# A new order of all engines, mask copies moved, fillers of 256 columns, the last product in two halves

## The chip, the cores and the metric

The kernel runs on one core of one Trainium2 chip. The metric is device time in microseconds (us), the median of the runs shown. Before the change it is 151.94 us, the median of three runs (150.77 to 152.38).

The engines have short names here: PE is TensorE (matrix products, with weight loads on their own row as PEld), DVE is VectorE, ACT is ScalarE, POOL is GpSimd, SP is SyncE. SP only issues transfers (DMAs) in this kernel. [...]

## The reference

Two stages follow each other. The first is linear attention with decay, for 4 batches, 8 heads, 768 positions and head dimension 64. In float32:

```python
for b in range(nb):                                   # blocks of 64 positions
    intra = einsum('bhic,bhjc->bhij', qb, kb) * Dmask  # Dmask[i, j] = lam ** (i - j), 0 above
    intra = einsum('bhij,bhjd->bhid', intra, vb)
    inter = einsum('bhid,bhde->bhie', qb * lam_pow, kv_state)
    out[:, :, sl] = intra + inter
    kv_state = lam_block * kv_state + einsum('bhsd,bhse->bhde', kb * rev_pow, vb)
```

The second is a gated feed-forward layer over the 512 features of each position:

```python
h = maximum(x @ w_in, 0)              # w_in is 512 x 1024
u, v = h[..., :512], h[..., 512:]
v_n = (v - mean(v)) / sqrt(var(v) + 1e-06)
v_s = einsum('ts,bsd->btd', w_spatial, v_n) + b_spatial[None, :, None]   # 768 x 768
out = (u * v_s) @ w_out               # w_out is 512 x 512
```

## The kernel before

**Tiling.** The 768 positions of a batch are three blocks of 256; with four batches there are twelve blocks, numbered 0 to 11. A block has all eight heads. Within a block, c is one of two chunks of 128 positions. The decay is split into factors of q and of v: `lq`, `lqn` and `lv` are tables of powers of lam, made at the start on ACT (LX, LT) from logarithms, so that the mask is only zeros and ones (`m01`).

**Steps.** A step is a short function; the string `ORDER` at the top lists all of them by token. A token has a name, its arguments, and a last letter for the engine: T for TensorE, D for DVE, A for ACT, P for POOL, S for SP. The steps for block n are:

- LK, LQ, LV load k, q and v of the block (512 KB each) through SP's queue. Each has three buffers, so load n goes to buffer n modulo 3 and waits until that buffer's earlier contents have been read.
- KC, QC cast k and q to bfloat16; VD multiplies v by its decay, one half of the heads in VD.n.0 and the other in VD.n.1.
- TK, TQ transpose k and q on TensorE by way of an identity matrix (line 328, eight products of 128 columns); EK, EQ take the results out of PSUM. For blocks 8 to 11, DK and DQ do this by transposing transfers, and QM stands for QC.
- SC makes scores (line 369, sixteen 64x64 products of 128 columns), MK masks them into `a_sb` (line 373, DVE).
- KV adds a chunk to the running state (line 385, sixteen products of 64 columns; it needs both halves of VD), SS copies the state out.
- AV makes the attention output of a chunk (lines 406 and 415); EX copies it out as `xT`. SY is a copy of two elements that keeps two engines apart.
- PV and PU multiply by the v half and the u half of w_in (line 444, four products of 512 columns; line 490, eight of 256); EV and EU are the relu. BN, RA, RD, VN normalise.
- WT transposes w_spatial once (line 502), EW copies it out. It needs all of w_spatial.
- PW multiplies by w_spatial for a batch (line 511, six products of 384 columns); GB adds the bias (line 516); GM multiplies by u (line 522) into `gT`.
- PO multiplies by w_out (line 528, four products of 512 columns), EO copies to one of four `o_sb` slots, ST stores. For the last tile of the last batch the copy and the store are in halves (EH, SH; line 541).
- WU are fillers: products of a constant tile whose result is never read (line 212). WU.24 is 24 of them. They stand on TensorE where it would wait.

**Weights.** w_in, w_spatial and w_out are loaded by POOL's queue (WI.0 the v half and WI.1 the u half of w_in, WS.0 and WS.1 of w_spatial, WO), with a cast to bfloat16 on the way. Ahead of each stands a gate GT.x.n: POOL copies one element out of buffer n modulo 3 of k, q or v (x = 0, 1, 2), and so can't go on until that buffer is loaded:

```python
def after(e, x, n):
    nc.gpsimd.tensor_copy(out=seen, in_=(k_in, q_in, v_in)[x][n % NIN][0:1, H - 1, 0, 0:1])
```

**Order.** There is no loop: the kernel walks through `ORDER` and calls each step. Waits between engines are put in by the framework from what each step reads and writes. The order was written by a planner, with fillers where it left TensorE idle. So the order of the tokens is both each engine's queue and the order in which reads and writes of one buffer are tied to each other.

Of the kernel before, what the change touches and what calls it, by code (L numbers as in the profile page):

```python
# [16 lines left out]
LK.0.2.S lam.A pos.P LQ.0.2.S LV.0.2.S LK.1.2.S msk.P WU.-8.T LB.5.T LN.5.A LL.D idn.P LQ.1.2.S LX.A LT.0.A  # L17
KC.0.2.P LV.1.2.S WU.24.T TK.0.4.T QC.0.2.D EK.0.4.A WU.10.T TQ.0.5.T LQ.2.2.S LT.1.A EQ.0.5.D GT.2.0.P WI.0.P
mkc.D WU.12.T SC.0.1.2.T LK.2.2.S SC.0.0.0.T VD.0.0.P MK.0.1.2.D KC.1.2.A VD.0.1.P MK.0.0.0.D LV.2.2.S WU.21.T
TK.1.2.T QC.1.2.D EK.1.2.D WU.11.T TQ.1.6.T AV.0.0.3.T LK.3.2.S EQ.1.6.D WU.4.T KV.0.0.T SS.0.0.A WU.2.T  # L20
SC.1.0.0.T VD.1.1.P SC.1.1.5.T LT.2.A AV.0.1.3.T MK.1.0.0.D KV.0.1.T GT.1.0.P WI.1.P MK.1.1.5.D VD.1.0.P
SS.0.1.A EX.0.1.4.A EX.0.0.3.D LQ.3.2.S WU.23.T AV.1.0.0.T KV.1.0.T PV.0.1.5.T QC.2.2.A SS.1.0.D LQ.4.2.S
WU.3.T TQ.2.4.T EV.0.1.5.A AV.1.1.0.T EQ.2.4.D GT.0.2.P WS.0.P KC.2.2.A PV.0.0.3.T EX.1.0.0.D GT.2.1.P WS.1.P
EX.1.1.1.A TK.2.2.T BN.0.1.D EV.0.0.3.A PV.1.1.6.T EK.2.2.D KV.1.1.T BN.0.0.D EV.1.1.6.A SC.2.1.0.T SC.2.0.4.T
PV.1.0.3.T LK.4.2.S MK.2.1.0.D RA.0.A VD.2.1.P MK.2.0.4.D WU.9.T PU.0.0.6.T SS.1.1.A VD.2.0.P EV.1.0.3.A
PU.0.1.0.T BN.1.0.D AV.2.0.1.T EU.0.1.0.A RD.0.D BN.1.1.D WU.4.T KV.2.0.T PU.1.0.3.T SS.2.0.A BS.S VN.0.0.A
AV.2.1.1.T KC.3.2.P PU.1.1.4.T EX.2.0.1.D EX.2.1.2.A EU.1.0.3.A EU.0.0.6.D PV.2.1.0.T RA.1.A EU.1.1.4.A
RD.1.0.D TK.3.3.T VN.0.1.D EV.2.1.0.A VN.1.0.D PV.2.0.1.T VN.1.1.D EK.3.3.A BN.2.1.D PU.2.0.4.T LV.3.2.S
EV.2.0.1.A BN.2.0.D EU.2.0.4.A QC.3.2.P WT.4.3.T WT.0.0.T LK.5.2.S EW.4.3.A WT.2.2.T EW.0.0.D WT.5.4.T
EW.2.2.A WT.3.6.T QC.4.2.P EW.5.4.D WT.1.5.T TQ.3.1.T RA.2.A EW.3.6.A LQ.6.2.S RD.2.0.D PU.2.1.3.T EQ.3.1.D  # L30
EW.1.5.A TQ.4.6.T VN.2.0.D EU.2.1.3.A VN.2.1.D SC.3.1.4.T LQ.5.2.S EQ.4.6.D KC.4.2.A SC.3.0.0.T PW.0.1.1.2.T
MK.3.0.0.D PW.0.0.0.3.T LV.4.2.S GB.0.1.1.2.D MK.3.1.4.D TK.4.0.T GM.0.1.1.P PW.0.1.0.6.T VD.3.1.P
GB.0.0.0.3.D LK.6.2.S PW.0.0.1.2.T GB.0.1.0.6.D GM.0.0.0.P EK.4.0.D PW.0.3.1.6.T VD.3.0.P PW.0.2.0.4.T
GB.0.3.1.6.D GM.0.1.0.P LV.6.2.S GB.0.0.1.2.D KV.3.0.T GB.0.2.0.4.D LV.5.2.S AV.3.0.0.T GM.0.0.1.P SC.4.1.2.T
SS.3.0.A SC.4.0.5.T SY.3.0.D AV.3.1.0.T MK.4.0.5.D QC.5.2.P KV.3.1.T PW.0.3.0.4.T EX.3.1.1.A LQ.7.2.S
EX.3.0.0.A MK.4.1.2.D KC.5.2.A TQ.5.6.T VD.4.0.P PU.3.0.5.T EQ.5.6.D LK.7.2.S TK.5.2.T VD.4.1.P SS.3.1.D
EU.3.0.5.A PU.3.1.6.T GB.0.3.0.4.D EK.5.2.A QC.6.2.P KV.4.0.T EU.3.1.6.D AV.4.0.0.T LV.7.2.S SS.4.0.A
SC.5.1.2.T GT.1.1.P WO.P SC.5.0.4.T SY.4.0.A KV.4.1.T AV.4.1.0.T MK.5.0.4.D PV.3.1.6.T KC.6.2.P EX.4.1.1.A
LK.8.2.S EX.4.0.0.A MK.5.1.2.D PW.0.2.1.1.T EV.3.1.6.A VD.5.1.P TK.6.4.T LQ.8.2.S TQ.6.5.T GM.0.3.0.P EK.6.4.D
PV.4.1.6.T EQ.6.5.D QC.7.2.A VD.5.0.P PU.4.1.0.T BN.3.1.D EV.4.1.6.A VD.6.1.P PU.4.0.2.T GB.0.2.1.1.D SS.4.1.A  # L40
EU.4.1.0.A BN.4.1.D VD.6.0.P PV.3.0.6.T EU.4.0.2.A LQ.9.2.S KV.5.0.T GM.0.2.0.P EV.3.0.6.D AV.5.0.0.T SS.5.0.A
SC.6.1.2.T SC.6.0.4.T SY.5.0.D KC.7.2.D KV.6.0.T AV.5.1.0.T PV.4.0.6.T MK.6.0.4.D EX.5.0.0.A EX.5.1.1.A
TK.7.0.T MK.6.1.2.D EV.4.0.6.A PO.0.1.1.T VD.7.1.P EK.7.0.A BN.3.0.D PV.5.1.4.T GM.0.3.1.P EO.0.1.1.A BN.4.0.D
PV.5.0.5.T RA.3.A ST.0.1.S EV.5.1.4.A VD.7.0.P LV.8.2.S RD.3.0.D PU.5.1.6.T EV.5.0.5.A GM.0.2.1.P TQ.7.3.T
BN.5.0.D EU.5.1.6.A PO.0.0.5.T QM.8.1.P SS.6.0.A BN.5.1.D PO.0.2.4.T EO.0.0.5.A EQ.7.3.D RA.5.A AV.6.0.0.T
ST.0.0.S VN.3.0.D EO.0.2.4.A KV.6.1.T LK.10.2.S SC.7.0.5.T SY.6.0.D RD.5.0.D SC.7.1.2.T SS.6.1.A KC.8.2.P
LK.9.2.S AV.6.1.0.T MK.7.0.5.D RA.4.A KV.7.0.T PO.0.5.4.T LV.9.2.S EX.6.0.0.A EX.6.1.1.A QM.8.0.P MK.7.1.2.D
PU.5.0.0.T SS.7.0.A VD.8.1.P RD.4.D KV.7.1.T EU.5.0.0.A AV.7.0.1.T PO.0.3.5.T VD.8.0.P VN.5.1.D VN.4.1.A
PV.6.0.0.T SY.7.1.A LV.11.2.S VN.4.0.D VN.5.0.D PV.6.1.6.T LQ.10.2.S EV.6.0.0.A SS.7.1.D VN.3.1.D EO.0.3.5.A
AV.7.1.1.T KV.8.0.T ST.0.3.S PW.1.0.1.5.T EX.7.1.2.A DQ.8.S EV.6.1.6.A EX.7.0.1.A PW.1.1.1.0.T VD.9.1.P  # L50
BN.6.1.D EO.0.5.4.A DK.8.S PV.7.1.6.T VD.9.0.P GB.1.1.1.0.D BN.6.0.D PU.6.1.2.T QM.9.0.P GB.1.0.1.5.D RA.6.A
PU.7.1.4.T EV.7.1.6.A QM.9.1.P KC.9.2.A BN.7.1.D PU.7.0.1.T SS.8.0.A GM.1.1.1.D PV.7.0.6.T DK.9.S EU.7.1.4.D
PW.1.3.1.3.T RD.6.D EV.7.0.6.A ST.0.2.S EU.6.1.2.A DQ.9.S QM.10.0.P BN.7.0.D PO.0.4.4.T EU.7.0.1.A
GB.1.3.1.3.D VN.6.1.A PW.1.0.0.6.T GM.1.0.1.P ST.0.5.S EO.0.4.4.D RA.7.A PU.6.0.5.T GB.1.0.0.6.D RD.7.D
SC.8.0.3.T LV.10.2.S GM.1.0.0.P EU.6.0.5.A KV.9.0.T SC.8.1.0.T MK.8.0.3.D LQ.11.2.S PW.1.2.1.6.T SS.9.0.A
QM.10.1.P MK.8.1.0.D PW.1.1.0.2.T GM.1.3.1.P PW.1.2.0.4.T GB.1.2.1.6.D GB.1.1.0.2.D AV.8.0.0.T GM.1.1.0.P
GB.1.2.0.4.D SC.9.1.2.T KV.9.1.T SY.8.0.D SC.9.0.5.T MK.9.1.2.D AV.8.1.0.T GM.1.2.1.P PW.1.3.0.4.T EX.8.0.0.A
DQ.10.S GM.1.2.0.P EX.8.1.1.D VN.7.0.A PO.1.3.0.T GB.1.3.0.4.D VN.7.1.A LK.11.2.S PV.8.1.1.T GM.1.3.0.P
VN.6.0.A PV.8.0.4.T EO.1.3.0.A VD.10.1.P EV.8.1.1.A ST.1.3.S PO.1.0.2.T QM.11.1.P EV.8.0.4.A BN.8.1.D
PO.1.1.1.T EO.1.0.2.A VD.10.0.P BN.8.0.D PO.1.5.0.T MK.9.0.5.D QM.11.0.P RA.8.A EO.1.1.1.A PU.8.0.3.T  # L60
KC.10.2.A ST.1.1.S RD.8.D ST.1.0.S PU.8.1.4.T VN.8.0.D ST.0.4.S VN.8.1.A DK.10.S PO.1.4.6.T EU.8.1.4.A
PW.2.0.1.1.T EU.8.0.3.A SS.9.1.A EO.1.5.0.A PW.2.1.1.3.T GB.2.0.1.1.D ST.1.5.S GM.2.0.1.P PW.2.0.0.2.T
GB.2.1.1.3.D KC.11.2.D GM.2.1.1.P PO.1.2.5.T GB.2.0.0.2.D DK.11.S PW.2.2.1.4.T EO.1.2.5.A GM.2.0.0.P
EO.1.4.6.A AV.9.0.0.T KV.10.0.T ST.1.4.S SC.10.1.2.T SY.9.0.D GB.2.2.1.4.D SC.10.0.5.T SS.10.0.A AV.9.1.0.T
# [12 lines left out]
GB.3.2.0.3.D ST.2.5.S ST.2.4.S GM.3.2.0.D PW.3.3.1.4.T GB.3.2.1.2.D PO.3.1.6.T GM.3.2.1.D GB.3.3.1.4.D
PO.3.0.3.T EO.3.1.6.A GM.3.3.1.P PO.3.2.1.T ST.3.1.S EO.3.0.3.A PO.3.5.2.T ST.3.0.S EO.3.2.1.A PO.3.3.5.T
ST.3.2.S EO.3.5.2.A PO.3.4.6.T EO.3.3.5.A ST.3.5.S ST.3.3.S EH.3.4.6.0.A EH.3.4.6.1.D SH.3.4.0.A SH.3.4.1.S
"""  # L80


@with_exitstack
def kernel(
    ctx: ExitStack,
    tc: tile.TileContext,
    q: bass.AP,
    k: bass.AP,
# [9 lines left out]
    P = 128  # L98
# [147 lines left out]
    def c_mask2(e):  # L246
        for c in range(2):
            rows = slice(c * Q64, (c + 1) * Q64)
            nc.vector.tensor_copy(out=m01[rows], in_=mfull[rows, :, :, rows])  # L249
# [335 lines left out]
```

## Time and profile before

| What | Before |
|---|---|
| median of three runs | 151.94 us (150.77 to 152.38) |
| the profiled execution, its own time | 153.37 us |
| its span, first to last instruction | 151.6 us |
| busy TensorE, DVE, ACT, POOL | 139.0, 101.3, 86.0, 79.6 us |
| DMA moved, mean rate over the span | 30.74 MB, 203 GB/s |
| TensorE instructions: products, weight loads | 2157, 2157 |
| of these products, fillers | 131 |
| first WT product starts | 38.08 us |
| last PO group starts | 142.63 us |

Lines of the timeline give the start in us from the beginning of the span, the time to the end of the group in us, the engine, the line of the kernel, the operation, what it writes and reads, the tile sizes and types, and how many instructions were merged. In brackets stand the idle time of the engine ahead of the group and what ended it. `ps` is PSUM, used in eight banks; the last argument of most TensorE tokens is the bank.

### The profile page before, as it was taken

What the parts mean: (1) busy time and instruction counts of PE and PEld (TensorE: products, weight loads), DVE (VectorE), ACT (ScalarE), POOL (GpSimd) and SP (SyncE); (2) the same over time, 40 slices, a digit from 0 to 9 for tenths busy, and PEclk for the clock granted to TensorE, in tenths of its full rate; (3) what the DMA queues carried; (4) which work ended last, traced back from release to release, by engine and by line L of the source; (5) the groups of instructions that cost most, each with busy time, mean ns of one, the idle gap of its engine ahead of it and who ended that gap; (6) DMA issues with size and microseconds to landing.
All of it is one profiled execution on the core that took longest, in us unless ns stands there. A gap on an engine that the chain in (4) does not pass through costs nothing.

```text
span 151.6 us, 5030 instructions
## 1 busy us (share of the span) xinstructions
PE 139.0 (92%) x2157; PEld 94.3 (62%) x2157; DVE 101.3 (67%) x189; ACT 86.0 (57%) x160; POOL 79.6 (52%) x90
## 2 busy tenths in 40 slices
PE   7795787999999995999999999899999999999990
PEld 6794675676975773776655756646576757555540
DVE  2159575958797964887893899946569828725601
ACT  6780356759940664658858562298353739760261
POOL 7464634505029959949370967695478050019310
PEclk9999999999999999999999999999999999999999
DMA  3999999999999799983799999587757000006355
GB/s 95 299 290 254 282 254 279 218 227 311 299 289 251 207 292 263 273 221 91 207 280 270 238 263 244 158 158 268 198 147 134 6 4 2 0 36 241 143 208 208
DMA packets 52041, 30.74 MB, mean 203 GB/s; under 512 B 9522, under 2 KB 48946, under 8 KB 52018
## 3 DMA queue, kind: packets, MB, share of 16 engines
q1 hardware_dynamic: 49488, 27.53, 68.8%
q0 software_dynamic: 2384, 2.75, 10.5%
q8 instruction: 17, 0.28, 0.8%
q10 hardware_dynamic: 146, 0.13, 0.3%
q14 instruction: 6, 0.05, 0.1%
HBM read 24.77 MB, written 6.29 MB: 205 GB/s over the span
## 4 chain that ended last, share of the span: by engine, by line
PE 74%; DVE 13%; DMA 3%; issue 3%; ACT 2%; POOL 2%; DVEq 0%; ACTq 0%
PE ps L511 16%; PE ps L528 13%; PE ps L444 13%; PE ps L490 12%; PE ps L328 5%; DVE a_sb L373 3%; PE ps L415 3%; DMA k_in<-in_k_dram 3%; PE ps L369 3%; PE ps L385 3%; PE ps L212 3%; DVE vsb L516 2%; PE ps L406 2%; PE ps L502 1%; DVE m L249 1%
## 5 line engine op out<-in xcount | busy, mean ns | idle before, releaser
L522 POOL TENSOR_TENSOR gT<-vsb,uT 128x384 bf16<-128x384 f32 x28 | 30.5, 1110 | 32.9 <-DVE vsb L516 20.1
L511 PE MATMUL ps<-wt_sb,vn 128*128 128x384 bf16 x192 | 33.9, 327 | 0.0
L314 POOL TENSOR_TENSOR vd<-v_in,lv 128x512 bf16<-128x512 f32 x24 | 24.8, 1046 | 12.3 <-PE ps L511 5.0
L373 DVE TENSOR_TENSOR a_sb<-ps,m 128x1024 bf16<-128x1024 f32 x24 | 28.5, 1216 | 2.7 <-PE ps L369 2.5
L511 PEld LDWEIGHTS <-vn 128*128 128x128 bf16 x192 | 18.2, 98 | 12.9
L444 PE MATMUL ps<-win_sb,xT 128*128 128x512 bf16 x96 | 24.1, 380 | 2.1 <-DVE a_sb L373 2.1
L516 DVE TENSOR_TENSOR vsb<-ps,bsp 128x384 f32<-128x384 f32 x32 | 17.3, 549 | 10.5 <-PE ps L511 7.2
L490 PE MATMUL ps<-xT,win_sb 128*128 128x256 bf16 x192 | 23.8, 273 | 0.0
L528 PE MATMUL ps<-wout_sb,gT 128*128 128x512 bf16 x96 | 22.9, 380 | 0.0
L459 DVE BATCH_NORM_STATS2 st<-vh 128x6 f32<-128x512 bf16 x24 | 16.4, 684 | 9.3 <-ACT vh L449 9.1
L490 PEld LDWEIGHTS <-win_sb 128*128 128x128 bf16 x192 | 18.4, 98 | 4.3
L449 ACT ACTIVATE vh<-ps 128x512 bf16<-128x512 f32 x23 | 13.7, 596 | 12.0 <-PE ps L444 11.8
L174 ACT ACTIVATE o_sb<-ps 128x512 f32<-128x512 f32 (+1 forms) x23 | 13.2, 587 | 12.5 <-PE ps L528 11.9
L174 ACT ACTIVATE xT<-ps 128x512 bf16<-128x512 f32 x18 | 10.2, 596 | 11.0 <-PE ps L415 11.0
L444 PEld LDWEIGHTS <-xT 128*128 128x128 bf16 x96 | 8.8, 98 | 10.5 <-issue 2.3
L528 PEld LDWEIGHTS <-gT 128*128 128x128 bf16 x96 | 9.0, 98 | 9.5
L449 ACT ACTIVATE uT<-ps 128x512 bf16<-128x512 f32 x21 | 12.2, 596 | 4.7 <-PE ps L490 4.6
L174 ACT ACTIVATE s_sb<-ps 128x256 bf16<-128x256 f32 x16 | 6.1, 381 | 14.3 <-PE ps L385 14.2
L212 PE MATMUL ps<-warm 128*128 128x128 bf16 x131 | 12.0, 255 | 2.1 <-DVE warm L210 1.1
L212 PEld LDWEIGHTS <-warm 128*128 128x128 bf16 x131 | 10.3, 117 | 2.9 <-DVE warm L210 1.1
L415 PE MATMUL ps<-a_sb,vd 64*64 64x128 bf16 x384 | 10.5, 218 | 1.0 <-issue 1.0
L369 PE MATMUL ps<-qT,kT 64*64 64x128 bf16 x384 | 8.8, 218 | 0.4 <-DVE vsb L516 0.4
(71 smaller groups left out, 172.8 us busy)
## 6 DMA issues: line engine op xcount, KB each, us to landing
k_in<-in_k_dram SPq DMA_DIRECT2D x12, 512.0 KB, 7.2
q_in<-in_q_dram SPq DMA_DIRECT2D x12, 512.0 KB, 8.1
v_in<-in_v_dram SPq DMA_DIRECT2D x12, 512.0 KB, 6.7
out_dram<-o_sb SPq DMA_DIRECT2D x23, 256.0 KB, 2.3
wsp_raw<-in_moe_w_spatial_dram POOLq DMA_DIRECT2D x2, 576.0 KB, 11.2
win_sb<-in_moe_w_in_dram POOLq DMA_DIRECT2D x2, 512.0 KB, 9.6
wout_sb<-in_moe_w_out_dram POOLq DMA_DIRECT2D x1, 512.0 KB, 7.8
bsp<-in_moe_b_spatial_dram SPq DMA_DIRECT2D x1, 384.0 KB, 8.2
```

Of the source, the lines that this page charges most:

```text
L174: nc.scalar.activation(out=o, in_=i, func=AF.Copy)
L212: nc.tensor.matmul(out=bank(SB)[:, 4 * D:4 * D + P], lhsT=warm, rhs=warm, start=(n < 0 and x == 0), stop=True, skip_group_check=True)
L314: vec(e).tensor_tensor(out=vd[n % NCA].rearrange("p (o i w) m d -> p o i (w m) d", o=2, i=2)[o], in0=v_in[n % NIN].rearrange("p (o i w) m ...
L373: nc.vector.tensor_tensor(out=a_sb[n % NA][:, i].rearrange("p o w j x -> p (o w) (j x)"), in0=bank(b, 2).rearrange("p o (w y) -> p (o w) y ...
L444: nc.tensor.matmul(out=bank(b), lhsT=x[:, c, g], rhs=win_sb[:, g, DH:DFF], start=(g == 0), stop=(g == NCH - 1))
L449: nc.scalar.activation(out=o, in_=i, func=AF.Relu)
L459: nc.vector.bn_stats(out=st6[p2][:, t], in_=vh[p2][:, t])
L490: nc.tensor.matmul(out=pu[:, f2].rearrange("p (c x) -> p c x", c=2), lhsT=win_sb[:, g, f * P:(f + 1) * P], rhs=x[:, :, g, :], start=(g == ...
L511: nc.tensor.matmul(out=bank(b)[:, 0:HW], lhsT=vn[bb % 2][:, s, f * P:(f + 1) * P], rhs=wt_sb[:, s, i * HW:(i + 1) * HW], start=(s == 0), s ...
L516: nc.vector.tensor_tensor(out=vsb[(bb * 4 + f) % NVS][:, i * HW:(i + 1) * HW], in0=bank(b)[:, 0:HW], in1=bsp[:, i * HW:(i + 1) * HW], op=A ...
L522: vec(e).tensor_tensor(out=gT[bb % 2][:, f, cols].rearrange("p (a y m) -> p a y m", m=2, y=Q64), in0=vsb[(bb * 4 + f) % NVS][:, cols].rear ...
L528: nc.tensor.matmul(out=bank(b), lhsT=gT[bb % 2][:, f, t * P:(t + 1) * P], rhs=wout_sb[:, f, :], start=(f == 0), stop=(f == NCH - 1))
```

## The change

All of `ORDER` is replaced by another order of the same computation; the sets of products on TensorE ahead of the first WT are the same. The head of it, old and new:

```diff
-LK.0.2.S lam.A pos.P LQ.0.2.S LV.0.2.S LK.1.2.S msk.P WU.-8.T LB.5.T LN.5.A LL.D idn.P LQ.1.2.S LX.A LT.0.A
-KC.0.2.P LV.1.2.S WU.24.T TK.0.4.T QC.0.2.D EK.0.4.A WU.10.T TQ.0.5.T LQ.2.2.S LT.1.A EQ.0.5.D GT.2.0.P WI.0.P
-mkc.D WU.12.T SC.0.1.2.T LK.2.2.S SC.0.0.0.T VD.0.0.P MK.0.1.2.D KC.1.2.A VD.0.1.P MK.0.0.0.D LV.2.2.S WU.21.T
-TK.1.2.T QC.1.2.D EK.1.2.D WU.11.T TQ.1.6.T AV.0.0.3.T LK.3.2.S EQ.1.6.D WU.4.T KV.0.0.T SS.0.0.A WU.2.T
-SC.1.0.0.T VD.1.1.P SC.1.1.5.T LT.2.A AV.0.1.3.T MK.1.0.0.D KV.0.1.T GT.1.0.P WI.1.P MK.1.1.5.D VD.1.0.P
-SS.0.1.A EX.0.1.4.A EX.0.0.3.D LQ.3.2.S WU.23.T AV.1.0.0.T KV.1.0.T PV.0.1.5.T QC.2.2.A SS.1.0.D LQ.4.2.S
-WU.3.T TQ.2.4.T EV.0.1.5.A AV.1.1.0.T EQ.2.4.D GT.0.2.P WS.0.P KC.2.2.A PV.0.0.3.T EX.1.0.0.D GT.2.1.P WS.1.P
...
+LK.0.2.S lam.A pos.P LQ.0.2.S LK.1.2.S LQ.1.2.S WU.-8.T LB.4.T LN.4.A LL.D LX.A LV.0.2.S LT.0.A KC.0.2.P
+LV.1.2.S idn.P LT.1.A WU.25.T TK.0.5.T QC.0.2.P msk.P LK.2.2.S EK.0.5.A WU.4.T TQ.0.4.T EQ.0.4.D GT.1.0.P
+WI.0.P mkc.A KC.1.2.D LQ.2.2.S WU.6.T SC.0.0.1.T SC.0.1.5.T TK.1.3.T MK.0.0.1.D QC.1.2.P EK.1.3.A LV.2.2.S
+WU.5.T TQ.1.0.T LT.2.A VD.0.0.D VD.0.1.P EQ.1.0.D LK.3.2.S MK.0.1.5.D WU.9.T SC.1.0.0.T KV.0.0.T VD.1.0.P
+SS.0.0.A MK.1.0.0.D WU.3.T SC.1.1.5.T AV.0.0.3.T GT.0.0.P WI.1.P KV.0.1.T SS.0.1.A SY.0.3.D MK.1.1.5.D
+VD.1.1.P WU.3.T AV.0.1.3.T KV.1.0.T EX.0.0.3.A AV.1.0.1.T LQ.3.2.S SS.1.0.A SY.1.1.D EX.0.1.4.A WU.2.T
+KV.1.1.T AV.1.1.1.T KC.2.2.P EX.1.1.2.A WU.2.T PV.0.1.3.T LQ.4.2.S EX.1.0.1.A GT.0.2.P WS.0.P TK.2.0.T
+EV.0.1.3.A QC.2.2.D PV.0.0.5.T GT.2.1.P WS.1.P EK.2.0.A BN.0.1.D TQ.2.1.T PV.1.1.6.T EV.0.0.5.D EQ.2.1.D
...
```

The crowded part on TensorE around the fourth and fifth block, and the end, in the new order:

```diff
...
+PU.3.0.0.T GB.0.3.0.4.D VD.4.1.P EQ.5.2.D TK.5.5.T EU.3.0.0.A PU.3.1.6.T GM.0.2.0.P LQ.7.2.S EK.5.5.A KV.4.0.T
+GT.0.1.P WO.P AV.4.0.0.T EU.3.1.6.A SS.4.0.D SC.5.0.4.T SY.4.0.A QC.6.2.P LV.7.2.S SC.5.1.2.T KV.4.1.T
+MK.5.0.4.D AV.4.1.0.T PV.3.1.6.T EX.4.0.0.A LK.8.2.S MK.5.1.2.D EX.4.1.1.A PV.3.0.4.T EV.3.1.6.A VD.5.1.P
...
+ST.3.0.S EO.3.2.6.A PO.3.3.4.T ST.3.2.S EO.3.5.5.A PH.3.4.0.0.T PH.3.4.1.1.T EO.3.3.4.A ST.3.5.S ST.3.3.S
+EH.3.4.0.0.A EH.3.4.1.1.D SH.3.4.0.A SH.3.4.1.S
```

In numbers of steps: fillers go from 131 in twelve groups to 71 in eleven. EK moves from four on DVE and four on ACT to eight on ACT; EX on DVE goes from six to two; KC on ACT from six to three; GM on DVE from four to seven (POOL 28 to 25); VD on DVE from none to two. The weights' gates change from GT.2.0, GT.1.0, GT.0.2, GT.2.1, GT.1.1 to GT.1.0, GT.0.0, GT.0.2, GT.2.1, GT.0.1, for WI.0, WI.1, WS.0, WS.1 and WO.

The functions that change:

```diff
-    warm = sb([P, P], BF16, "warm")
+    warm = sb([P, T2], BF16, "warm")
...
-            nc.tensor.matmul(out=bank(SB)[:, 4 * D:4 * D + P], lhsT=warm, rhs=warm, start=(n < 0 and x == 0), stop=True,
+            nc.tensor.matmul(out=bank(SB)[:, 4 * D:8 * D], lhsT=warm[:, 0:P], rhs=warm, start=(n < 0 and x == 0), stop=True,
                              skip_group_check=True)
...
     def c_mask(e):
+        nc.gpsimd.memset(eps_t, 1e-6)
         nc.gpsimd.memset(mfull, 1.0)
...
             rows = slice(c * Q64, (c + 1) * Q64)
-            nc.vector.tensor_copy(out=m01[rows], in_=mfull[rows, :, :, rows])
-        nc.vector.memset(eps_t, 1e-6)
+            copy(e, m01[rows], mfull[rows, :, :, rows])
...
+    def p_h(e, bb, t, b, x):
+        half = slice(x * (DM // 2), (x + 1) * (DM // 2))
+        for f in range(NCH):
+            nc.tensor.matmul(out=bank(b)[:, half], lhsT=gT[bb % 2][:, f, t * P:(t + 1) * P],
+                             rhs=wout_sb[:, f, half], start=(f == 0), stop=(f == NCH - 1))
+
```

The mask copies (mkc) are now on ACT, behind the copy of the first kT. The last tile's product is made by PH in two halves, in banks 0 and 1, and EH copies each half from its own bank.

## The prediction

> **What bounds the kernel now.** I read the page's shares of the engines first, then stretches of the span, then TensorE in order of time, then GpSimd. Page, parts 1 to 3:
>
> ```profile
> PE 139.0 (92%) x2157; PEld 94.3 (62%) x2157; DVE 101.3 (67%) x189; ACT 86.0 (57%) x160; POOL 79.6 (52%) x90
> ...
> DMA  3999999999999799983799999587757000006355
> ...
> q8 instruction: 17, 0.28, 0.8%
> ```
>
> TensorE (PE) is busy 92% of the span; the DMA engines are at nine tenths from the second to the thirteenth slice (to 49 us). The stretches before and after the transposes of w_spatial (steps WT) are the natural cut: both orders put the same products of TensorE ahead of WT.
>
> ```profile
> 0.00:38.08 38.08, 31.75 (x565) 25.36 (x565) 23.58 (x43) 23.43 (x42) 18.29 (x30) 1.00 1.08 251
> 38.08:151.60 113.52, 107.22 (x1593) 68.95 (x1592) 77.72 (x147) 62.58 (x118) 61.30 (x60) 1.00 0.71 187
> ```
>
> (Columns: length; busy us and count of PE, weight loads, DVE, ACT, POOL; clock; DMA share; GB/s.) After WT, TensorE is nearly dense. The head is loose: seven transposing steps at 0.45 us, six SC and five KV at 0.24, six AV at 0.46, six PV and five PU at 0.87, durations from the chain's rows, make 18 us of 38. TensorE in order of time:
>
> ```profile
> 10.75 1.35 PE L212 MATMUL ps<-warm 128*128 128x128 bf16 x21
> ...
> 19.82 1.44 PE L212 MATMUL ps<-warm 128*128 128x128 bf16 x23 [0.48 <-ACT s_sb L174]
> ...
> 21.55 0.41 PE L385 MATMUL ps<-vd,kc 64*64 64x64 bf16 x16
> ...
> 24.81 0.41 PE L415 MATMUL ps<-a_sb,vd 64*64 64x128 bf16 x13 [0.97 <-issue]
> ...
> 58.60 1.04 PE L444 MATMUL ps<-win_sb,xT 128*128 128x512 bf16 x4 [2.12 <-DVE a_sb L373]
> ...
> 96.23 0.42 PE L369 MATMUL ps<-qT,kT 64*64 64x128 bf16 x16 [0.40 <-DVE vsb L516]
> ```
>
> The reader sees three late stops. The first two are of one kind, although the second is put down to DVE. Counting TensorE's instructions in order of start, 707 precede the first stop and 1987 the second[...]. The packet records of queue q8 show 16,384-byte fetches at 22.38 (0.97 us long) and 55.98 (1.19 us); each stop ends 1.45 us after its fetch. These are waits for **instruction fetch**, 3.09 us together. 21.55 is the second block's first KV product, the milestone used below. GpSimd:
>
> ```profile
> 15.11 0.64 POOL L253 COPY seen<-q_in 1x1 f32<-1x1 f32 x1
> 15.70 0.80 POOL L257 DMA_DIRECT2D win_sb<-in_moe_w_in_dram  x1
> 16.51 1.06 POOL L314 TENSOR_TENSOR vd<-v_in,lv 128x512 bf16<-128x512 f32 x1
> 21.17 0.17 POOL L253 COPY seen<-k_in 1x1 f32<-1x1 f32 x1 [3.60 <-DMA k_in<-in_k_dram]
> ...
> 56.74 0.18 POOL L253 COPY seen<-q_in 1x1 f32<-1x1 f32 x1 [1.82 <-DMA q_in<-in_q_dram]
> ```
>
> A gate (GT, line 253) is a copy of one element on GpSimd that holds a weight load back. The last line is the gate GT.1.1 of buffer q_in_1. Loads 1, 4 and 7 use that buffer; load 7 stands ahead of the gate in the order, and the trace's landing of load 7 is at 56.69. So **a gate waits for the last load of its buffer that stands ahead of it**, not for the load whose number it bears.
>
> [...] fillers stand 107 ns apart up to about 10.6 us, 4.4 us after dense work began at 6.2, and 63 ns in the row at 19.82. [...] loads land 1.8 us apart, but 5.19 us apart (14.05, 19.24) where w_in's first half flows.
>
> **The change part by part.**
>
> *Fillers.* 131 of 128 columns become 71 of 256. At 63 ns before and an estimated 109 ns (256/128 of 54 ns, the gap less a few ns) that is 8.2 against 7.7 us, and 120 instructions fewer. They fill waits, so their price on the path is nothing while data is what the head waits for; uncovered, it is 0.5 us less.
>
> *Mask copies to ScalarE, eps memset to GpSimd.* Two copies took 2.12 us on DVE ("DVE m L249", mean 1052 ns), ahead of the first masked scores (12.14). On ACT the nearest row is 0.38 us (s_sb, 128x256); bounds 0.38 to 1.05 each. With k0 ready on GpSimd at 6.15, both lq tables on ACT ahead of kT (4 x 0.42 us each, to about 8.8), kT at 9.8 and the mask at 10.6, the first MK starts at 10.65: 1.5 us earlier.
>
> *Loads.* k1, q1 go ahead of v0, which lands fifth (12.29, not 8.67). Then VD.0 ends about 13.4, KV.0.0 about 14.0, AV.0.1 about 16.9: a lead over before of some 2 to 3 us.
>
> *The gates.* Now the step that decides. The second half of w_in (WI.1) sat behind GT.1.0 (q0, long landed). It is put behind GT.0.0, buffer k_in_0, and LK.3 (load k3, same buffer) stands ahead of it. By the rule above it waits for **k3**, the tenth load. Without WI.1 between them: 14.05 (sixth) + 4 x 1.8 + 3.39 us for w_in's first half = 24.6. Behind the gate on GpSimd stand WI.1's issue and VD.1.1, half of the second block's scaled v, which KV.1.0 needs[...]. 24.65 + 0.18 (gate) + 0.87 (issue, L257 mean 865 ns) + 1.05 (L314) = 26.75 for KV.1.0, against 21.55: 5.2 us later, after 9.8 us of idle TensorE. KC.2 and both w_spatial issues follow on the same queue.
>
> From KV.1.0 to WT the new order has: 3 KV 0.72, 4 AV 1.84, 6 PV 5.22, 3 transposing steps 1.35, 2 SC 0.48, 5 PU 4.37, 8 fillers 0.88 = 14.9 us (durations from the chain's rows; a PV of four 0.87, a PU of eight 0.87, eight transposes 0.45). The cold array adds: the 64-wide steps first, some 1.8 us, hardly slow (32 scores took 0.57 us cold at 10.18); then 2.6 us at half rate lose 1.3, say 1.4. Bounds 0 to 2.2. WT at 26.75 + 14.9 + 1.4 = **43.0**, not 38.08. The data allow it: WI.1 issued at 24.8 lands 9.2 to 10.0 us later as both halves did before (34 to 34.9; first PU about 35.3), and the w_spatial halves, 7.9 us of flow behind it, about 41.6 to 42.4.
>
> *After WT.* Products are the same; 113.5 us less what goes. The fetch stop at 58.6: the crowded run KV.4 to AV.4.1 is still there[...] I take a stop of 0.3, bounds 0 to 2. So -2.12 + 0.3. The stop of 0.40 goes (SC.9 uses other banks): -0.40. Unsized new waits of an order untried: +0.7, bounds 0 to 2.
>
> *Engine swaps and store order.* By counts times means ACT gains about 3 us, DVE loses as much; at 57% and 67% neither becomes the bound, TensorE's products cover them. In SP's queue DK, DQ and the stores change places by one or two entries; stores are waited for by four o_sb slots alone, 0.4 us in all before. Cost nothing; if the cover is gone, each late read of a bank costs its 0.6 us.
>
> *Last product in halves (PH).* Eight matmuls of 256, about 0.44 us a half, for four of 512, 0.87: equal on TensorE. ACT and DVE now read different banks. Before, DVE's half (148.47) waited for ACT's (148.06); at 97.5 the two write one xT tile from different banks at once, so the bank was the reason: -0.45, bounds 0 and -0.6.
>
> Sum against the profiled span: 43.0 + 113.5 - 2.12 + 0.3 - 0.40 + 0.7 - 0.45 = 154.5, or +2.9 on 151.6. That execution took 153.37, 1.77 around its span and 1.43 over the median of 151.94. Added to the median: **154.8 us**, own range 153 to 156.5.
>
> **Rivals.** (A) *The gate is no wait* (faster): GT.0.0 finds k0 landed. Then WI.1 and w_spatial are issued as early as before, land about 35.2, WT comes at 35.5 instead of 43.0: 154.8 - 7.5 = 147.3. For it: too few fillers (2 and 2) stand round KV.1.0 for a 10 us hole. Against: the row at 56.74. It decides if GT.0.0 ends under 20 us. (B) *Fetch stops move instead of going, and the cold lasts*: +2 [...] +0.8 cold: 157. [...] (C) *The head loses less and the rest gains more*: WT at 41.6, when the last w_spatial lands, no new waits: 154.8 - 1.4 - 0.7 - 0.3 = 152.4, about no change.
>
> **Chances.** Main 0.65, A 0.11, B 0.13, C 0.11. A measurement here tells about 1% from nothing, 1.5 us. Slower by over that (from 153.5): main but for its lower edge, and B, 0.75; within: C and that edge, 0.13; faster: A and a little, 0.12. The range leaves out A and B's far end: 150.8 to 157.8.
>
> **What would show it.** In the changed profile: the copy at line 253 waiting for k_in until 24 to 25; PE idle about 9 us before a KV product near 26.8; PV rows with doubled spacing after it; WT near 43; no stop of 2 us in the middle; the two last o_sb copies side by side. Wrong if the gate ends early, or if the stretch after WT is longer than 113.

## The result and the profile after

The changed kernel takes **158.81 us** (median of four runs, 157.76 to 159.15) against 152.04 us (four runs, 150.77 to 152.38) for the kernel before: a ratio of **1.045 [1.037, 1.053]**. It is slower, as forecast, but 4.0 us above the forecast of 154.8 and 1.0 us above the end of its range (157.8). The profiled execution took 158.55 us, its span 156.8. (Ratios here leave disturbed executions out, so they need not be the quotient of the medians beside them.)

The page of the changed kernel, parts 1 to 3 (engines; clock granted to TensorE in 40 slices; DMA in the same slices; the queue of instruction fetches):

```profile
PE 138.6 (88%) x2088; PEld 92.9 (59%) x2101; DVE 99.5 (63%) x191; ACT 88.1 (56%) x166; POOL 77.4 (49%) x88
...
PEclk9999975599999999999999999999999999999999
DMA  4999999999987359999399999972949200035155
...
q8 instruction: 16, 0.26, 0.7%
```

TensorE is busy as long as before in a span 5.2 us longer. Its clock row, all nines before, now has three low slices (7, 5 and 5 tenths), from 19.6 to 31.4 us. The two stretches, cut at the first WT product (columns as in the prediction):

```profile
0.00:44.67 44.67, 32.16 (x503) 23.52 (x505) 20.16 (x39) 24.27 (x46) 20.00 (x33) 0.89 1.06 247
44.67:156.80 112.13, 106.41 (x1587) 69.40 (x1596) 79.39 (x153) 63.81 (x121) 57.41 (x55) 1.00 0.70 176
```

So the head costs 6.59 us more (44.67 for 38.08), and everything after it 1.39 less (112.13 for 113.52). The loss is all ahead of WT. TensorE in order of time:

```profile
18.36 0.29 PE L386 MATMUL ps<-vd,kc 64*64 64x64 bf16 x8
27.70 0.32 PE L386 MATMUL ps<-vd,kc 64*64 64x64 bf16 x5 [9.05 <-POOL vd L315]
...
36.66 1.91 PE L491 MATMUL ps<-xT,win_sb 128*128 128x256 bf16 x16
...
44.67 2.20 PE L503 MATMUL ps<-ident,wsp_raw 128*64 128x128 bf16 x72
...
71.30 0.25 PE L386 MATMUL ps<-vd,kc 64*64 64x64 bf16 x5 [0.66 <-POOL vd L315]
...
81.48 1.47 PE L529 MATMUL ps<-wout_sb,gT 128*128 128x512 bf16 x6 [0.36 <-issue]
```

Half of KV.1.0's sixteen products run at 18.36. The other half needs VD.1.1 and starts at 27.70, after 9.05 us of idle TensorE. The stops of 2.12 and 0.40 us of the kernel before are gone; 0.66 and 0.36 have come. GpSimd shows what VD.1.1 stood behind:

```profile
14.03 1.04 POOL L315 TENSOR_TENSOR vd<-v_in,lv 128x512 bf16<-128x512 f32 x1 [0.66 <-DMA v_in<-in_v_dram]
25.30 0.18 POOL L254 COPY seen<-k_in 1x1 f32<-1x1 f32 x1 [10.22 <-DMA k_in<-in_k_dram]
25.77 0.81 POOL L258 DMA_DIRECT2D win_sb<-in_moe_w_in_dram  x1 [0.30 <-issue]
26.59 1.05 POOL L315 TENSOR_TENSOR vd<-v_in,lv 128x512 bf16<-128x512 f32 x1
```

The gate GT.0.0 ends a wait of 10.22 us at 25.30; load k3 landed at 25.17. Only then are the second half of w_in and both halves of w_spatial issued (25.77, 28.69, 29.94). They land at 36.38, 40.10 and 43.72, the last of them 0.95 us ahead of WT. The end of the program:

```profile
152.22 1.04 PE L535 MATMUL ps<-wout_sb,gT 128*128 128x256 bf16 x8
...
153.32 0.38 ACTq L548 DMA_DIRECT2D out_dram<-o_sb  x1
153.35 0.42 DVE L177 COPY o_sb<-ps 128x256 f32<-128x256 f32 x1 [3.68 <-ACT o_sb L175]
153.80 0.33 SPq L548 DMA_DIRECT2D out_dram<-o_sb  x1
```

DVE's half starts 0.09 us after TensorE's end at 153.26, and the last store is issued 0.54 us after it, against 0.95 before.

### The profile page after: what moved, and what is told of

It is laid out like the page before. It is cut to its first block, busy times and chain, and to the rows that moved or that the text cites. A ratio compares the mean times of both kernels' runs of the same rounds, so it can differ in the third digit from the quotient of the medians.

```text
span 156.8 us, 4932 instructions
## 1 busy us (share of the span) xinstructions
PE 138.6 (88%) x2088; PEld 92.9 (59%) x2101; DVE 99.5 (63%) x191; ACT 88.1 (56%) x166; POOL 77.4 (49%) x88
## 3 DMA queue, kind: packets, MB, share of 16 engines
q0 software_dynamic: 2384, 2.75, 10.1%
## 4 chain that ended last, share of the span: by engine, by line
PE 51%; issue 1%; DVE 0%; DVEq 0%
PE ps L512 15%; PE ps L529 13%; PE ps L445 8%; PE ps L491 8%; PE ps L416 2%; PE ps L386 2%; PE ps L370 1%; PE ps L407 1%; PE ps L329 1%; PE ps L535 1%; DVE o_sb L177 0%; DVEq L177 0%
## 5 line engine op out<-in xcount | busy, mean ns | idle before, releaser
L523 POOL TENSOR_TENSOR gT<-vsb,uT 128x384 bf16<-128x384 f32 x25 | 28.1, 1138 | 43.6 <-DVE vsb L517 30.7
L512 PEld LDWEIGHTS <-vn 128*128 128x128 bf16 x192 | 18.4, 98 | 12.4
L315 POOL TENSOR_TENSOR vd<-v_in,lv 128x512 bf16<-128x512 f32 x22 | 22.7, 1042 | 4.1 <-PE ps L416 2.5
L445 PE MATMUL ps<-win_sb,xT 128*128 128x512 bf16 x88 | 22.5, 382 | 0.8 <-issue 0.6
L529 PE MATMUL ps<-wout_sb,gT 128*128 128x512 bf16 x87 | 21.7, 379 | 0.7 <-issue 0.5
L386 PE MATMUL ps<-vd,kc 64*64 64x64 bf16 x320 | 9.3, 197 | 9.8 <-POOL vd L315 9.7
L450 ACT ACTIVATE vh<-ps 128x512 bf16<-128x512 f32 x21 | 12.5, 595 | 8.4 <-PE ps L445 8.2
L175 ACT ACTIVATE xT<-ps 128x512 bf16<-128x512 f32 x22 | 12.2, 594 | 5.9 <-PE ps L416 5.9
L386 PEld LDWEIGHTS <-kc 64*64 64x64 bf16 x320 | 7.5, 111 | 12.5 <-issue 12.4
L213 PE MATMUL ps<-warm 128*128 128x256 bf16 x71 | 12.8, 336 | 2.3 <-DVE warm L211 1.3
L175 ACT ACTIVATE kT<-ps 128x1024 bf16<-128x1024 bf16 x8 | 8.2, 1023 | 7.3 <-PE ps L329 7.2
```

The lines of the kernel that those rows point to most:

```text
L175: nc.scalar.activation(out=o, in_=i, func=AF.Copy)
L315: vec(e).tensor_tensor(out=vd[n % NCA].rearrange("p (o i w) m d -> p o i (w m) d", o=2, i=2)[o], in0=v_in[n % NIN].rearrange("p (o i w) m ...
L386: nc.tensor.matmul(out=pkv[row(o), u], lhsT=kc[n % NCA][row(c), u, m, o, :], rhs=vd[n % NCA][row(c), 4 * o + u, m, :], start=new and u == ...
L445: nc.tensor.matmul(out=bank(b), lhsT=x[:, c, g], rhs=win_sb[:, g, DH:DFF], start=(g == 0), stop=(g == NCH - 1))
L450: nc.scalar.activation(out=o, in_=i, func=AF.Relu)
L512: nc.tensor.matmul(out=bank(b)[:, 0:HW], lhsT=vn[bb % 2][:, s, f * P:(f + 1) * P], rhs=wt_sb[:, s, i * HW:(i + 1) * HW], start=(s == 0), s ...
```

## The experiments

Three questions. Is the gate's place behind load k3 the cause? What sets WT once the gate waits: TensorE's own chain behind VD.1.1 (as predicted), or the late weights? And what were the stops in the middle, and what becomes of the time when they go?

### 1. Nothing but the gate, in the changed kernel

Load k3 is moved behind the gate in the order, so that k0 is the last load of that buffer ahead of it.

```diff
-... EQ.1.0.D LK.3.2.S MK.0.1.5.D ... AV.0.0.3.T GT.0.0.P WI.1.P KV.0.1.T ...
+... EQ.1.0.D MK.0.1.5.D ... AV.0.0.3.T GT.0.0.P WI.1.P LK.3.2.S KV.0.1.T ...
```

> The changed kernel with load k3 placed behind the gate GT.0.0 in the order (SP's own queue is unchanged), so that the gate reads load k0, long landed. Gate theory: the copy of line 254 ends near 15.3 us instead of 25.5, the first KV of the second block comes at about 18.5 instead of 27.7, WT at about 36 instead of 44.7, time about 150.5 us (149 to 152.5). Rival, the rest of the new order costs the time: 156 or more, with WT late all the same.

Measured: 150.53 us (150.12 to 151.22), ratio to before 0.990 [0.983, 0.997], 8.3 us below the changed kernel; span 148.4. GpSimd, then TensorE, in order of time:

```profile
15.04 0.18 POOL L254 COPY seen<-k_in 1x1 f32<-1x1 f32 x1
...
56.41 0.18 POOL L254 COPY seen<-k_in 1x1 f32<-1x1 f32 x1 [5.00 <-DMA k_in<-in_k_dram]
```
```profile
34.82 2.20 PE L503 MATMUL ps<-ident,wsp_raw 128*64 128x128 bf16 x72
...
58.43 0.62 PE L329 MATMUL ps<-ident,qc 128*128 128x128 bf16 x8 [1.92 <-POOL qc L179]
```

The gate no longer waits, VD.1.1 follows it, and WT comes at 34.82, 9.85 us earlier. **The whole loss of the change is this one load's place in the order.** The gain is less than those 9.85 us: the stretch after WT is 113.6 us, not 112.1. The second gate, GT.0.1 ahead of w_out, now holds GpSimd for 5.00 us for load k7, and QC.6 behind it makes TensorE stop for 1.92.

### 2. Nothing but the gate, in the kernel before

One token: the gate ahead of WI.1 reads the buffer of k0 and k3 instead of q0's. LK.3 stands ahead of it there too.

```diff
-... AV.0.1.3.T MK.1.0.0.D KV.0.1.T GT.1.0.P WI.1.P MK.1.1.5.D VD.1.0.P
+... AV.0.1.3.T MK.1.0.0.D KV.0.1.T GT.0.0.P WI.1.P MK.1.1.5.D VD.1.0.P
```

> The kernel before with one token changed: the gate of w_in's second half reads buffer k_in_0 behind load k3 (GT.0.0 for GT.1.0). Gate theory: GpSimd waits until about 25.2 us, WT moves from 38 to about 44, time +5 to +6.5 us, 157 to 158.5. Rival, the gate is worth little and the new order is the loss: under 154.

Measured: 161.98 us (161.23 to 163.14), ratio 1.065 [1.054, 1.076]: nearly 10 us, well over the 5 to 6.5 expected; span 160.7. GpSimd, then TensorE, in order of time:

```profile
25.23 0.17 POOL L253 COPY seen<-k_in 1x1 f32<-1x1 f32 x1 [10.01 <-DMA k_in<-in_k_dram]
```
```profile
27.63 0.64 PE L415 MATMUL ps<-a_sb,vd 64*64 64x128 bf16 x16 [7.67 <-POOL vd L314]
...
45.70 2.20 PE L502 MATMUL ps<-ident,wsp_raw 128*64 128x128 bf16 x72
...
66.12 1.04 PE L444 MATMUL ps<-win_sb,xT 128*128 128x512 bf16 x3 [2.01 <-DVE a_sb L373]
```

The gate ahead of WI.1, which ran at 15.11 without a wait in the kernel before, now ends its wait at 25.23, 10.1 us later. VD.1.0 stands behind it on GpSimd, so AV.1.0, which needs it, starts at 27.63 for 21.32, after a hole of 7.67 us. Behind the hole the clock is low (8, 5, 5 and 8 tenths in the slices from 20 to 36 us), and WT comes 7.62 later (45.70 for 38.08). The weights land late as well, but TensorE has no wait for them on this way: w_in's second half landed at 34.25 and its first product starts at 37.24; the second half of w_spatial landed at 42.06, 3.64 us before WT. Here TensorE's own chain alone sets WT. The stretch after WT took 115.0, 1.5 more, with a second low spell of the clock (8 and 7 tenths) from 64 to 72 us. So the mechanism is confirmed in a second kernel, and its price was underestimated here as in the prediction.

### 3. What sets WT: VD.1.1 freed, the weights still late

```diff
-... AV.0.0.3.T GT.0.0.P WI.1.P KV.0.1.T SS.0.1.A SY.0.3.D MK.1.1.5.D VD.1.1.P WU.3.T ...
+... AV.0.0.3.T VD.1.1.P GT.0.0.P WI.1.P KV.0.1.T SS.0.1.A SY.0.3.D MK.1.1.5.D WU.3.T ...
```

> The changed kernel with VD.1.1 moved ahead of the gate, gate and loads as they are. Theory of the prediction (what stands behind the gate on GpSimd, VD.1.1, is what TensorE waits for, and sets the loss): KV.1.0 at about 18.5, time down by 4 us or more, to about 153 to 155. Rival (the weights issued behind the gate land late, and set the loss by themselves): KV.1.0 early, but the first PU not before 36 and WT not before 43, when the second half of w_spatial lands; time 157.3 to 158.5.

Measured: 157.32 us (156.18 to 158.69), ratio 1.032 [1.023, 1.041]; span 157.0. TensorE in order of time:

```profile
27.63 1.03 PE L329 MATMUL ps<-ident,kc 128*128 128x128 bf16 x8 [5.83 <-POOL kc L179]
...
36.94 1.92 PE L491 MATMUL ps<-xT,win_sb 128*128 128x256 bf16 x16 [2.58 <-DMA win_sb<-in_moe_w_in_dram]
...
44.96 2.20 PE L503 MATMUL ps<-ident,wsp_raw 128*64 128x128 bf16 x72
```

KV.1.0 now runs at about 18.4, nine microseconds earlier, and **WT does not move** (44.96 for 44.67). KC.2, the next entry behind the gate on GpSimd, stops TensorE in its turn; and the first PU product waits 2.58 us for w_in's second half, which landed at 36.89. From there to WT are 8.02 us, as in the changed kernel (36.66 to 44.67 is 8.01). So TensorE's chain behind VD.1.1, which the prediction took for the one path, can be shortened without moving WT: the landing of w_in's second half binds at the same moment. A third path is hardly shorter: the second half of w_spatial landed at 44.24, 0.72 us before WT. The median is 1.5 us below the changed kernel's, not the 4 us or more of the prediction's account. The profiled execution is the longest of the four (158.69 us, the others 156.18 to 157.53), so where those are shorter is not shown. Weights issued early with VD.1.1 alone held back was not tried, since w_in's flow would, by the author's estimate, move the landing of k3 too (in the kernel before loads landed 5.19 us apart where its first half flowed, for 1.8).

### 4. What the cold array costs: fillers in the hole

```diff
-... VD.1.1.P WU.3.T AV.0.1.3.T KV.1.0.T EX.0.0.3.A ...
+... VD.1.1.P WU.3.T AV.0.1.3.T WU.80.T KV.1.0.T EX.0.0.3.A ...
```

> The changed kernel, gate and all, with 80 fillers of 256 columns in the hole ahead of KV.1.0, to keep the array at full clock through it. If the cold array costs what the prediction gave it, 1.4 us on the way from KV.1.0 to WT, and nothing else is late there, WT comes at about 43.2. If the second half of w_in sets the time by its landing (36.4), the steps ahead of the first PU shrink by some 1.5 us and PU waits instead: WT at 44.3 to 44.8 and the total unchanged, 157.5 to 159.

Measured: one time, 160.1 us; span 158.4. TensorE in order of time:

```profile
27.91 0.25 PE L386 MATMUL ps<-vd,kc 64*64 64x64 bf16 x5 [1.16 <-POOL vd L315]
...
37.22 1.92 PE L491 MATMUL ps<-xT,win_sb 128*128 128x256 bf16 x16 [1.66 <-DMA win_sb<-in_moe_w_in_dram]
...
45.24 2.20 PE L503 MATMUL ps<-ident,wsp_raw 128*64 128x128 bf16 x72
```

With the array warm (granted clock 1.00 from 27.91 to 45.24), KV.1.0 to the fillers ahead of PU takes 7.04 us (27.91 to 34.95) instead of 8.51 (27.70 to 36.21): the cold costs **1.47 us** in this one execution, 1.11 of it ahead of the first PV (27.70 to 30.84 against 27.91 to 29.94). None of it is gained: TensorE waits 1.66 us for w_in instead. This is the same verdict as experiment 3, from the other side. The 80 fillers (160 instructions, products and weight loads) also shift the count of TensorE's instructions at every later step, and two stops appear that the changed kernel lacks, 0.71 us at 63.80 and 0.93 at 86.55, after 1985 and 2750 recorded instructions; the first count is that of the stop of 2.12 us in the kernel before, 1987, but for two (some records are missing).

### 5. The fetch stop: the kernel before, unchanged, and with wide fillers

> The kernel before, profiled once more, to see how far its own profiled execution (153.37 us, span 151.6) stands from its median of 152.04. If the two stops of TensorE in it, 0.97 us at instruction 707 and 2.12 us at instruction 1987, are waits for instruction fetch[...], they stand at the same counts again, with lengths that follow the start of the fetch; a span of about 150.3 to 151.6. Rival, stops put down to DVE: they move with DVE's work and not with the count.

Measured: one time, 154.76 us; span 153.1. The clock row of the page, then TensorE in order of time:

```profile
PEclk9999857999999999999999999999999999999999
```
```profile
60.17 1.04 PE L444 MATMUL ps<-win_sb,xT 128*128 128x512 bf16 x3 [2.20 <-DVE a_sb L373]
```

The large stop comes again, 2.20 us, after 1983 recorded instructions. The early one, at 707, does not. This execution has a half-speed spell from 17.8 to 24.7 us, ahead of it, in which 23 fillers took 2.61 us for 1.44; WT comes at 39.55. Whether the spell kept that stop away was not shown. The kernel before, too, varies in its idle head.

Then the fillers of the kernel before become 256 wide, 75 for 131, and nothing else (the fillers' product and its tile as in the change):

```diff
-WU.-8.T ... WU.24.T ... WU.10.T ... WU.12.T ... WU.21.T ... WU.11.T ... WU.4.T ... WU.2.T ... WU.23.T ... WU.3.T ... WU.9.T ... WU.4.T
+WU.-5.T ... WU.14.T ... WU.6.T ... WU.7.T ... WU.12.T ... WU.6.T ... WU.2.T ... WU.1.T ... WU.13.T ... WU.2.T ... WU.5.T ... WU.2.T
```

> The kernel before with its fillers 256 columns wide and fewer of them (75 for 131, each group of the same length in time), nothing else. That takes 112 instructions from TensorE ahead of the crowded part, so the edge at count 1987 falls on KV.5.0 instead of PV.3.1[...]. Fetch theory: the stop of 2.1 us ahead of PV.3.1 is gone[...]; time 149.5 to 151. Rival, DVE's masks end that stop: it stays near 2 us, time 151.5 to 152.5.

Measured: 151.64 us (150.2 to 155.59, 20 runs) against 152.61 (48 runs), ratio 0.995 [0.992, 0.998]: 0.6 us more than the upper end of what was expected. With 112 instructions fewer (products and weight loads) ahead of it, the PV that stopped for 2.1 us no longer stops. It starts at 54.37, while DVE's two masks run until 56.39, so it never needed them. What this gives is passed on, as GpSimd and TensorE show in order of time:

```profile
56.97 0.18 POOL L253 COPY seen<-q_in 1x1 f32<-1x1 f32 x1 [4.10 <-DMA q_in<-in_q_dram]
```
```profile
54.37 1.04 PE L444 MATMUL ps<-win_sb,xT 128*128 128x512 bf16 x3
...
58.99 0.62 PE L328 MATMUL ps<-ident,kc 128*128 128x128 bf16 x8 [2.61 <-POOL kc L178]
```

The w_out gate waits for load q7 as before; TensorE is now there sooner and stops 2.61 us for KC.6, queued on GpSimd behind that gate. The stop went with the instruction count (1987 and 1983 in the two profiles of the kernel before, gone with 112 fewer), not with DVE's `a_sb`, which the view named; and behind it stood a second wait of the same size.

### 6. Following the wait at the w_out gate

From experiment 1, QC.6 is moved ahead of the gate, so that it isn't queued behind it:

```diff
-GT.0.1.P WO.P AV.4.0.0.T ... SY.4.0.A QC.6.2.P LV.7.2.S ...
+QC.6.2.P GT.0.1.P WO.P AV.4.0.0.T ... SY.4.0.A LV.7.2.S ...
```

> The changed kernel with the gate GT.0.0 reading k0 (as in the run with load k3 behind the gate), and besides QC.6 moved ahead of the second gate of this kind, GT.0.1, which there held GpSimd for 5.0 us until load k7 landed and TensorE for 1.92 us at TQ.6. The stop of 1.92 us and the one of 0.66 us at KV.6 go: 147.8 to 149 us. If a fetch of instructions or late loads take its place: 149.5 or more.

Measured: 151.29 us (149.47 to 153.3, 20 runs), ratio 0.994 [0.990, 0.997]: no gain over experiment 1, and a miss. GpSimd and TensorE again:

```profile
58.11 0.18 POOL L254 COPY seen<-k_in 1x1 f32<-1x1 f32 x1 [4.18 <-PE ps L491]
```
```profile
62.18 0.38 PE L386 MATMUL ps<-vd,kc 64*64 64x64 bf16 x13 [2.68 <-POOL vd L315]
```

The gate still waits for load k7, which landed at 58.06 (the view names a TensorE product instead), 1.7 us later than in experiment 1. The entries behind it, VD.5.1 and then VD.5.0, which ends at 62.1, take QC.6's place as what TensorE waits for. To move one entry past the gate did not help while the gate waited (4.18 us); the next in the queue were as late. On top of this one, TK.3 and its copy were moved behind the first three WT steps, to start WT ahead of the 1.1 us wait for KC.3:

```diff
-... VN.1.0.A TK.3.5.T BN.2.0.D LK.4.2.S WT.2.0.T EK.3.5.A EU.2.0.4.D WT.4.3.T QC.3.2.P WT.3.6.T
+... VN.1.0.A BN.2.0.D LK.4.2.S WT.2.0.T EU.2.0.4.D WT.4.3.T QC.3.2.P WT.3.6.T TK.3.5.T EK.3.5.A
```

> As the run with QC.6 moved, and besides TK.3 placed behind the first three WT, since it waited 1.1 us for the cast of k3 while w_spatial had landed (33.6). 0.5 to 1.1 us less than that run: 147 to 148.3. If WT then waits for w_spatial or for banks instead, no difference.

Measured: 151.83 us (149.76 to 152.79), ratio 0.988 [0.984, 0.993]; the profiled execution had a half-speed slice in its middle. WT starts at 34.10, but TensorE stops 0.66 us three microseconds later, for the copy of that same kT. The 147 to 148.3 us expected were missed, and against experiment 6 this is inconclusive.

### 7. Opening the w_out gate itself

On experiment 6, the gate reads a buffer whose last load ahead of it is an earlier one: v5 in the first kernel, k6 in the second.

```diff
-QC.6.2.P GT.0.1.P WO.P AV.4.0.0.T
+QC.6.2.P GT.2.2.P WO.P AV.4.0.0.T
```

> As the run with QC.6 moved (gate of w_in's second half on k0), and the gate of w_out reads v5 (GT.2.2) instead of k7, so that VD.5.1 behind it can go as soon as its own data are there (54.6 in that run). The stop of 2.68 us at KV.5.0 shrinks to about 0.3; w_out is issued near 55 and lands near 63.5, when the first PO wants it: 147 to 148.5 us. If w_out then comes late, the stop moves to the first PO: 149 or more.

```diff
-QC.6.2.P GT.0.1.P WO.P AV.4.0.0.T
+QC.6.2.P GT.0.0.P WO.P AV.4.0.0.T
```

> The same with w_out's gate on k6 (GT.0.0), landed before the gate is reached: w_out is issued near 54 and its 512 KB go ahead of loads v5 and k7, which land up to 3 us later. If these loads have room: 147 to 148.5, no stop at KV.5.0 over 0.5 us. If v5 becomes late by it: a stop of 1 to 2 us at KV.5.0, 149 to 150.

And the same for the kernel before with the wide fillers of experiment 5:

```diff
-SC.5.1.2.T GT.1.1.P WO.P SC.5.0.4.T
+SC.5.1.2.T GT.0.0.P WO.P SC.5.0.4.T
```

> The kernel before with fillers 256 wide and fewer, and w_out's gate on k6 (GT.0.0) instead of q7. In the run with wide fillers alone the fetch stop of 2.1 us at PV.3.1 was gone and TensorE waited 2.6 us for KC.6, which stood behind that gate on GpSimd. Theory: both stops are gone now, 2 to 3 us less than with wide fillers alone: 148.5 to 150. Rival, loads pushed back by w_out give the stop back: 151 to 152.

Measured, against 152.53 us (11 runs) before on the same chip:

| Kernel | median us (range) | ratio to before | span, WT, after WT |
|---|---|---|---|
| changed order, gate on v5 | 149.62 (148.34 to 152.22) | 0.979 [0.974, 0.984] | 147.1, 34.76, 112.34 |
| changed order, gate on k6 | 150.80 (147.72 to 151.96) | 0.977 [0.969, 0.985] | 149.3, 34.83, 114.5 |
| order before, wide fillers, gate on k6 | 149.37 (148.48 to 150.78) | 0.979 [0.975, 0.984] | 149.1, 37.28, 111.82 |

The gate on k6 doesn't wait at all in the order before, here in GpSimd's order of time, and both middle stops are gone; the largest left after WT is 0.40 us:

```profile
54.11 0.18 POOL L253 COPY seen<-k_in 1x1 f32<-1x1 f32 x1
```

All three are about 2% faster than the kernel before, and their medians are 5 to 6% below the changed kernel's; the ratio in the second row rests on two of its six executions. The first two medians are above the 147 to 148.5 us expected, the third lies within its 148.5 to 150. In the first, TensorE's wait of 2.68 us at KV.5.0, where 0.3 was expected, is gone altogether. One step on, KV.6.0 waits 0.49 us for VD.6.1 (0.65 in experiment 6), and a stop of 0.54 appears after 1729 recorded instructions. The new order shows no advantage over the old one with wide fillers and this gate open: the medians are 0.25 us apart, inside the intervals. The stretches of the third row come from the longest of its executions (150.78 us), so its 111.82 and 37.28 can't be set against those of the first row.

## Why the prediction was right in sign and short in size

**Right.** That a gate waits for the last load of its buffer ahead of it in the order, read from one row of the kernel before, held in both kernels (experiments 1 and 2). So did its copy's time (25.30 against 24.65), the hole (9.05 against 9.8), and that the fetch stop of 2.12 and the bank wait of 0.40 go. Two sizes fit by luck. What comes in their place was 0.36 + 0.66 for the 0.3 + 0.7 in the sum, but the 0.7 was a guess that named no wait. The cold array cost 1.47 against 1.4; that the clock would fall behind the hole was the author's estimate, from the slow start of the kernel before (fillers 107 ns apart at first, 56 later), and the changed kernel's row of 7, 5 and 5 tenths shows it. But 1.11 of the cost (experiment 4) fell on the 64-wide steps and the fillers among them, which the prediction called hardly slow. It had read the 32 scores at 10.18 as cold. In the kernel before, the fillers on both sides of them stand 56 ns apart and not 107, so the array was at full clock already, from 9.9 us on and not from 10.6. The 0.36 looks like a fetch stop: it ends 1.39 us after the end of a fetch at 78.92 (1.17 long), where the two of the kernel before ended 1.45 us after theirs. The 0.3 in the sum, for a fetch stop in the crowded run, was the author's estimate; the 0.36 came later, at 81.48. The rows of 0.16 us marked "issue" are no stops: each precedes a group short of a product whose weight load is there (the page has 13 more weight loads than products, so some product records are missing). Mask copies on ACT took 0.41 each, as guessed (0.38 to 1.05).

**Wrong.** The miss is 4.0 us in three terms.

- *The gates*, and with them WT at 43.0: measured 44.67, 1.67 us. KV.1.0 came 0.95 late (k3 landed at 25.17, not 24.6; a 0.30 us pause before the issue), and the 14.9 + 1.4 us behind it took 16.97. But the step fails more deeply than by these sizes. It followed TensorE's chain and let the data pass with "The data allow it": w_in's second half 9.2 to 10.0 us after issue, as in a head without the hole. It took 10.6 (25.77 to 36.38), w_spatial's second half 13.8 (29.94 to 43.72, not 42.4; 34.9 + 7.9 would have been 42.8). Experiments 3 and 4 showed, in their profiled executions, that the landing of w_in's second half alone gives WT at 45: with VD.1.1 freed, or the array warm, WT comes 8.0 us after it all the same. Two paths of equal length were taken for one.
- *After WT*: 112.13 for 111.55, 0.58 us. The half products did what was said as far as the issue of the last store (0.41 us earlier, -0.45 expected), but from that issue to the end of the span it took 3.00 us instead of 2.68, so 0.09 was left. The remaining 0.2 us shows as no stop and stays open.
- *The sum's last line*, 1.7 us. It added a difference of two profiled spans to a median. The profiled execution of before lay 1.43 us over its median, that of after 0.26 under its own. Experiment 5's first run (154.76, WT 1.5 us late from a half-speed spell) shows how far single executions of this kernel differ. The step had noted the 1.43, and then gave it no width in the range.

Together 1.67 + 0.58 + 1.7 = 3.95. Smaller steps: fillers of 128 columns stand 56 ns apart, not 63, on which nothing depended; masked scores started at 11.93, not 10.65, because DVE had KC.1's cast (1.50 us) in front; KV.0.0 at 14.84 for 14.0. Both leads died at the gate. Of the **rivals**, C was refuted by the landing of w_spatial at 43.72, not 41.6; B came nearest in time (157), but not by its mechanism: the cold was not longer, and its stop of 2 us didn't come. A was false for the changed kernel, but as an estimate of what an open gate gives it was good: WT 35.5 against the 34.82 of experiment 1. Its 147.3 us failed by 3.2. Of this, 1.4 is in the span (148.4 for 147.0), where the second gate took back part of the gain; the rest lies, as in the main sum, between span and median.

## What to carry to other kernels

A copy that stands in for "wait until this is loaded" waits for the last load into that rotating buffer issued ahead of it, and what is queued behind it on its engine waits too (10.22 us in the changed kernel, for k3, with VD.1.1 behind it): list, for each such gate, which load that is. When a wait delays both an engine's work and a transfer's issue, price both paths to their meeting point, and take the transfer's time from one issued under the same load (here 10.6 us, for the 9.2 to 10.0 assumed). When a stop is removed, look at once for what was just as late behind it; here only opening the gate freed what two other edits had merely passed on.

## What the runs showed of the hardware that was not expected

- TensorE's clock also fell after stops far shorter than the hole of 9.05 us. In the kernel of experiment 7 with the gate on k6, three products of 512 columns, 2 us after a gap of 1.71, took 1.48 us, where three in the changed kernel took 0.81 at full speed, and the clock row has a slice of 5 tenths from 78.4 to 82.1. TensorE in order of time:

```profile
77.33 0.31 PE L407 MATMUL ps<-qT,s_sb 64*64 64x128 bf16 x8 [1.71 <-ACT apart_A L175]
...
79.36 1.48 PE L445 MATMUL ps<-win_sb,xT 128*128 128x512 bf16 x3 [0.22 <-issue]
```

  It happened after stops of 1.32 and 0.64 us in the kernel with WT first (5 tenths from 64.0 to 67.8), and after 2.01 in experiment 2 (8 and 7 tenths from 64 to 72). But stops of 2.61 (experiment 5) and 2.68 (experiment 6) left every slice of the clock row at nine tenths or more. So the length of a single stop did not tell which, and what decides it was not shown.
- Fetches of instructions (queue q8) took 0.88 to 1.24 us in the changed kernel; those ahead of the two stops in the kernel before took 0.97 and 1.19. One stop came at the same instruction count in four executions, with other work at it in the last: after 1983 to 1987 recorded instructions in the kernel before (2.12 and 2.20 us), in experiment 2 (2.01) and in experiment 4 (0.71).
- In the changed kernel the three weight halves issued behind the gate (0.5 to 0.6 MB each), with SP's loads running beside them, took 10.6, 11.4 and 13.8 us to land; the first half of w_in, issued at 9.15, took 8.9.
